# A cached decode attention whose first weight load is issued as two halves, on two queues

## The chip, the cores and the metric

The kernel runs on one core of a Trainium2 chip. The metric is the device time of one execution in microseconds. Before the change it is 2558.99 us, the median of three runs from 2558.98 to 2559.40. "The profile" is one profiled execution of the same program on the chip; its trace holds the start and duration of every instruction and of the DMA engines' packets.

## The reference

Two independent blocks, A and B, of single-token attention over a cache; the outputs stand side by side. For each of them:

```python
B, Sq, D = 8, 1, 1024;  H, Sk, Dh = 32, 4096, 128      # all bf16
q = (x @ wq).reshape(B, Sq, H, Dh).transpose(0, 2, 1, 3)
scores = einsum("bhqd,bhkd->bhqk", q, k_cache) * Dh ** -0.5
o = einsum("bhqk,bhkd->bhqd", softmax(scores), v_cache)
out = o.transpose(0, 2, 1, 3).reshape(B, Sq, H * Dh) @ wo
```

The caches are read once and dominate: 8 x 32 x 4096 x 128 bf16 elements are 268 MB, and there are four of them (K and V of A and B). The weights `wq` and `wo` are 8.39 MB each.

## The kernel before, in words

**Tiles.** Every large load fills one of the three slots of `ring`, an SBUF buffer of 128 partitions and 64 KB per partition and slot. A K or V tile is 8 heads of one batch entry, 8.39 MB; there are 64 K tiles and 64 V tiles. A `wq` fills exactly one slot too: partition p holds the 8 rows 8p to 8p+7 of the matrix, 65,536 contiguous bytes of device memory.

**Order of the loads.** A list `plan` names the loads in order with their slots: `wq` of A (slot 1), K tile 0 (slot 0), `wq` of B (slot 2), then K tile n+1 and V tile n in turn, at the end the two `wo`. All are issued by SyncE, on its DMA queue, and each waits until the slot's last tenant has been used. `load_tiles` issues as far down the list as tenants allow. Between the first load and K tile 0 it also issues the two inputs x (8 partitions, 2 KB each), which lie in slot 2 until they have been transposed.

**The start.** TensorE transposes x once it has landed, VectorE copies the result (L525), TensorE projects it with `wq` of A (`make_q`, L334 and the helper's L36), ScalarE copies the query out of PSUM (L342), TensorE transposes that (L350), VectorE stores it (L354), and ScalarE and TensorE spread the query of one batch entry and 8 heads over the partitions (`qst` L361, `misc` L366, `qbc` L368). Then the loop over the 64 tiles begins.

**The loop.** A K tile is worked in four chunks: VectorE multiplies a chunk with `qbc` in place (`make_mul`, L379), adds the two halves of each row (L384), TensorE adds further with an identity matrix into PSUM (L395, L36), and VectorE reduces to scores (L405). Behind the fourth chunk come maximum, exponent (L417) and the product with V (L434), one tile later. After the last tile, the sums are normalised and multiplied with `wo`.

**How waits are written.** `_Program` keeps one list of operations per engine. An operation that others depend on counts up its engine's semaphore; a load counts up its slot's semaphore (`("t", w)`) by 16. `run(engine, part=(a, b))` emits operations a to b of an engine's list, with waits for the counts that they need. SyncE's first four operations (the first load, the two x, K tile 0) are emitted by a call of its own, ahead of the block in which each engine gets its program.

**Names.** q1 in the profile is SyncE's DMA queue; "SPq" stands for SyncE's issuing of a DMA. A "packet" is what one DMA engine moves at a time; in the large loads it is one partition's 65,536 bytes.

Of the kernel before, what the change touches and what calls it, by code (L numbers as in the profile page):

```python
# [59 lines left out]
class _Program:  # L60
# [13 lines left out]
    def add(self, eng, emit, deps=(), dma_key=None, moves=False):  # L74
        op = _Op(eng, emit, list(deps), dma_key, moves)
        if dma_key is not None:
            self.counts[dma_key] = self.counts.get(dma_key, 0) + 16
            op.token = (dma_key, self.counts[dma_key])
        for d in op.deps:
            if not (d.eng == "pe" and eng == "pe"):  # L80
                d.sig = True
        self.ops[eng].append(op)
        return op
# [32 lines left out]
    def run(self, engname, eng, sems, loop=None, part=(0, None)):  # L116
        ops = self.ops[engname]
        waits, known = self._waits(engname)

        def emit(op, at=lambda base, step: base):  # L120
            ins = op.emit(eng, at) if op.moves else op.emit(eng)
            if op.dma_key is not None:
                ins.then_inc(sems[op.dma_key], 16)
            elif op.sig:
                ins.then_inc(sems[op.eng], 1)

        def straight(lo, hi):
            for op, left in zip(ops[lo:hi], waits[lo:hi]):
                for key, val in left.items():
                    eng.wait_ge(sems[key], val)  # L130
                emit(op)

        start, end = part[0], len(ops) if part[1] is None else part[1]
        ahead = eng.mark_branch_hint_location() if engname in self.ahead else None
        for first, per, rounds in loop or ():
            at = [self.marks[first + per * i][engname] for i in range(rounds + 1)]
            straight(start, at[0])
            self._repeat(engname, eng, sems, ops, waits, known, emit, at, per, rounds, ahead)
            start = at[-1]
        straight(start, end)  # L140
# [32 lines left out]
def _build_kernel(nc, caches, out):  # L173
    B, Sq, D = caches[0][0].shape
    _, H, Sk, Dh = caches[0][1].shape
    NC = len(caches)
    assert B == 8 and Sq == 1 and Dh == 128 and Sk == 4096 and D == 1024 and H % 8 == 0 and 128 % H == 0
    DC = D // 128
# [16 lines left out]
    with es:  # L195
# [36 lines left out]
        sems = {e: es.enter_context(nc.semaphore(f"c_{e}")) for e in ENGINES[1:]}  # L232
# [4 lines left out]
        P = _Program()  # L237
        add = P.add

        def dma(out_ap, in_ap, key, deps, eng="sp"):  # L240
            return add(eng, lambda e: e.dma_start(out_ap, in_ap), deps, dma_key=key)  # L241

        def load_cache(to, n, side, key, deps):
            c = where(n)[0]
            size = HQ * Sk * Dh
            whole = caches[c][side].rearrange("b h s d -> (b h s d)")

            def emit(e, at):
                return e.dma_start(to, whole[bass.ds(at(n % (B * HB) * size, size), size)].rearrange("(p x) -> p x", p=128))
            return add("sp", emit, deps, dma_key=key, moves=True)  # L250
# [23 lines left out]
        opT, opMul, opEacc, opRed, opNgm, opExp = {}, {}, {}, {}, {}, {}  # L274
# [18 lines left out]
        def where(n):  # L293

            return n // (B * HB), n // HB % B, n % HB
# [7 lines left out]
        def load_tiles():  # L303
            while issued[0] < len(plan):
                if issued[0] == 1 and not op_x:
                    op_x.extend(dma(x_sb[:, c, :], caches[c][0].rearrange("b s d -> b (s d)"), ("x", 0), []) for c in range(NC))
                kind, n, w = plan[issued[0]]
                prev = before[issued[0]]
                dep = opUse.get(prev)
                if prev is not None and dep is None:  # L310
                    return
                to, key = ring[:, w, :], ("t", w)
                if kind in ("k", "v"):
                    opT[(kind, n)] = load_cache(to, n, 1 if kind == "k" else 2, key, [dep])
                elif kind == "wq":
                    opT[(kind, n)] = dma(to[:, 0:DC * H * Dh], caches[n][3].rearrange("(p k) n -> p (k n)", k=DC), key, [dep])
                else:
                    from_ = caches[n][4].rearrange("(p r) n -> p (r n)", r=H)
                    for i, (r0, r1) in enumerate(wo_cuts if n == NC - 1 else ((0, H),)):
                        opT[(kind, n, i)] = dma(to[:, r0 * D:r1 * D], from_[:, r0 * D:r1 * D], key if n < NC - 1 else ("w", i), [dep])  # L320
                issued[0] += 1
# [191 lines left out]


        load_tiles()

        def emit_xT(e):
# [14 lines left out]
        for n in range(NQ):  # L532
            P.mark(n)
            for r in range(NR):
                s = n * NR + r
                make_mul(s)
                if s >= LAG:
                    make_red(s - LAG)
                if r == LAG - 1 and n >= 1:
                    make_shift(n - 1)  # L540
                fold = make_fold(s)
                if r == LAG - 1 and n >= 1:
                    make_pm(n - 1)
                if n == 0 and r == NR - 1:
                    for c in range(1, NC):
                        make_q(c)
                        make_qT(c)
                if r == 2 and n >= 1:
                    make_pv(n - 1, 0, RG // 2)
                if r == 3 and n >= 1:  # L550
                    make_pv(n - 1, RG // 2, RG)
                    make_acc(n - 1)
                if r == 2 and n + 1 < NQ:
                    make_stage(n + 1)
                    make_qbc(n + 1)
                make_eacc(s, fold)
                load_tiles()
                if r == 3 and n >= 1:
                    make_ext(n - 1)
        P.mark(NQ)  # L560
        n = NQ - 1
# [4 lines left out]
        make_pv(n, 0, RG)  # L566
        make_acc(n)
        load_tiles()
        make_ext(n)
        make_norm(1)  # L570
# [7 lines left out]
        loops = {"pe": [(1, 2, (NQ - 2) // 2)], "dve": [(3, 2, (NQ - 4) // 2)], "act": [(3, HB, (NQ - 4) // HB)]}  # L578

        P.run("sp", nc.sync, sems, part=(0, 2 + NC))  # L580
        with nc.Block() as block:

            @block.sync
            def _(eng):
                P.run("sp", eng, sems, part=(2 + NC, None))

            @block.tensor
            def _(eng):
                P.run("pe", eng, sems, loops["pe"])

            @block.scalar
            def _(eng):
                P.run("act", eng, sems, loops["act"])

            @block.vector
            def _(eng):
                P.run("dve", eng, sems, loops["dve"])

            @block.gpsimd
            def _(eng):  # L600
                P.run("pool", eng, sems)
# [4 lines left out]
def bass_concat_heads__mha_block_cached__mha_block_cached__decode_kernel(  # L606
    nc, A_x, A_k_cache, A_v_cache, A_wq, A_wo, B_x, B_k_cache, B_v_cache, B_wq, B_wo, out,
):
    caches = [(A_x, A_k_cache, A_v_cache, A_wq, A_wo), (B_x, B_k_cache, B_v_cache, B_wq, B_wo)]
    _build_kernel(nc, caches, out)  # L610
# [28 lines left out]
```

## Time and profile before

| what | value |
|---|---|
| median of three runs | 2558.99 us |
| profiled execution: its span, first to last instruction | 2557.8 us |
| bytes moved by DMA, mean rate | 1107.48 MB, 433 GB/s |
| VectorE busy | 2170.2 us, 85% |
| TensorE busy | 1115.8 us, 44% |
| ScalarE busy | 130.3 us, 5% |
| first load: issued by SyncE at | 0.80 us, landing 22.2 us later |
| first product of VectorE on a K tile | 42.41 us |

The busy share of an engine is an average over the span. In the slices of the page each digit or number is one of 40 equal parts of the span. In a table of windows, a row has the stretch, its length, the busy time of TensorE's matmuls, its weight loads, VectorE, ScalarE and GpSimd with their counts, the granted clock of TensorE, the share of the 16 DMA engines, and GB/s. In a timeline, a row has the start, the duration, the engine, the line and operation with its tiles, and in brackets the idle time ahead of it with what ended it.

### The profile page before, as it was taken

The page shows a single profiled execution, that of the slowest core. Times are in us where ns is not written, and L with a number is a line of the kernel's source. Part 1 is how long each engine was busy: PE and PEld are TensorE (multiplying, and loading weights), DVE is VectorE, ACT ScalarE, POOL GpSimd, SP SyncE. Part 2 cuts the span into 40 slices and gives each one's busy share as a digit, 9 for nine tenths or more (in the row PEclk, how much of TensorE's full clock was granted, in tenths as well). Part 3 has the DMA queues.
Part 4 walks back from the last instruction along what each step waited for, and adds up shares of the span by engine and source line. Part 5 has one row for each costly group of instructions (what it writes and reads, how often), then busy time and mean ns, then how long its engine had stood idle before and what let it go on. Part 6 is the DMA issues. An engine that isn't in the chain of part 4 may idle for free.

```text
span 2557.8 us, 16927 instructions
## 1 busy us (share of the span) xinstructions
PE 1115.8 (44%) x7664; PEld 181.0 (7%) x5808; DVE 2170.2 (85%) x1036; ACT 130.3 (5%) x402; POOL 2.6 (0%) x15
## 2 busy tenths in 40 slices
PE   2443443443444444444444444444444434434444
PEld 0000000000000000000000000000000000000002
DVE  3798898898898898898898888988988988988983
ACT  1100000000000000000000000000000000000000
POOL 0000000000000000000000000000000000000000
PEclk7666776666766666767667767766666767667767
DMA  9999999999999999999999999999999999999999
GB/s 427 427 441 427 442 427 442 427 439 430 438 431 433 436 430 439 429 440 429 440 429 440 430 440 429 440 429 439 429 440 429 440 429 437 431 437 433 435 434 398
DMA packets 19551, 1107.48 MB, mean 433 GB/s; under 512 B 2184, under 2 KB 2248, under 8 KB 2520
## 3 DMA queue, kind: packets, MB, share of 16 engines
q1 hardware_dynamic: 19544, 1107.37, 99.9%
q8 instruction: 6, 0.10, 0.0%
q14 instruction: 1, 0.01, 0.0%
HBM read 1107.33 MB, written 0.03 MB: 433 GB/s over the span
## 4 chain that ended last, share of the span: by engine, by line
DMA 51%; DVE 28%; issue 16%; PE 4%; another core or an unknown queue 0%; ACT 0%; DVEq 0%; SPq 0%
DMA ring<-in_B_k_cache_dram 25%; DMA ring<-in_A_k_cache_dram 25%; DVE ring L379 10%; DVE ring L384 10%; DVE s_sb L405 4%; PE red L36 4%; DVE PM L422 3%; DMA ring<-in_B_wo_dram 2%; PE red L395 1%; DVE rmax L411 1%; DVE rtmp L412 0%; ACT PM L342 0%; DVEq L169 0%; SPq L241 0%
## 5 line engine op out<-in xcount | busy, mean ns | idle before, releaser
L379 DVE TENSOR_TENSOR ring<-ring,qbc 128x8192 bf16<-128x8192 bf16 x256 | 1131.7, 4421 | 300.7 <-DMA ring<-in_B_k_cache_dram 150.9
L395 PE MATMUL red<-ring,ident 128*128 128x512 bf16 x256 | 136.3, 532 | 1382.2 <-DVE ring L384 1382.2
L36 PE MATMUL red<-ring,ident 128*128 128x512 bf16 x1792 | 695.9, 554 | 0.0
L384 DVE TENSOR_TENSOR ring<-ring 128x4096 bf16<-128x4096 bf16 x256 | 582.1, 2274 | 0.0
L405 DVE TENSOR_REDUCE s_sb<-red 128x64 f32<-128x1024 f32 x256 | 311.8, 1218 | 3.4 <-PE red L36 3.4
L434 PE MATMUL pv<-ring,PM 128*32 128x512 bf16 x4096 | 273.8, 414 | 4.7 <-DVE PM L422 4.7
L422 DVE TENSOR_TENSOR PM<-pe,own_h 128x2048 bf16<-128x2048 bf16 x64 | 146.3, 2285 | 0.7 <-ACT pe L417 0.7
L395 PEld LDWEIGHTS red<-ring,ident 128*128 128x128 bf16 x256 | 25.9, 101 | 1653.2 <-DVE ring L384 1653.2
L434 PEld LDWEIGHTS pv<-ring,PM 128*32 128x32 bf16 x4096 | 103.6, 104 | 433.8 <-issue 360.9
L368 ACT ACTIVATE qbc<-misc 128x128 bf16<-128x128 f32 x64 | 17.8, 278 | 1087.0 <-PE misc L366 1087.0
L417 ACT ACTIVATE pe<-s_sb,ngm 128x256 bf16<-128x256 f32 x64 | 32.5, 508 | 465.1 <-DVE ngm L415 465.1
L442 ACT ACTIVATE accS<-pv 128x512 bf16<-128x512 f32 x64 | 38.2, 597 | 352.0 <-PE pv L434 352.0
L451 PEld LDWEIGHTS o<-accS,E 128*32 128x32 bf16 x1024 | 31.3, 100 | 193.3 <-issue 192.1
L451 PE MATMUL o<-accS,E 128*32 128x32 bf16 x1024 | 38.1, 185 | 0.7 <-ACT accS L442 0.7
L457 ACT ACTIVATE o_sb<-o 32x32 f32 (+1 forms) x64 | 11.9, 186 | 450.9 <-PE o L451 443.1
L411 DVE TENSOR_REDUCE rmax<-s_sb 128x1 f32<-128x256 f32 x64 | 26.9, 420 | 2.2
L361 ACT ACTIVATE qst<-qT 128x128 bf16 (+1 forms) x64 | 18.7, 293 | 2.3 <-DVE qT L354 2.3
L525 DVE COPY xT<-misc 128x128 bf16<-128x128 bf16 x1 | 0.2, 225 | 21.9 <-PE misc L521 21.9
L498 PE MATMUL proj<-ring,on_sb 128*32 128x256 bf16 x244 | 10.8, 350 | 15.4 <-DMA ring<-in_A_wo_dram 8.2
L412 DVE TENSOR_SCALAR rtmp<-half,rmax 128x32 f32<-128x32 f32 x64 | 15.5, 241 | 2.3
L354 DVE COPY qT<-misc 128x256 bf16<-128x256 bf16 x2 | 2.6, 1278 | 17.1 <-PE misc L350 17.1
L366 PE MATMUL misc<-ident,qst 128*128 128x128 bf16 x64 | 14.8, 232 | 1.7 <-ACT qst L361 1.7
(37 smaller groups left out, 82.6 us busy)
## 6 DMA issues: line engine op xcount, KB each, us to landing
ring<-in_B_wo_dram SPq DMA_DIRECT2D x1, 5120.0 KB, 32.7
ring<-in_B_wo_dram SPq DMA_DIRECT2D x1, 2048.0 KB, 37.2
ring<-in_B_wo_dram SPq DMA_DIRECT2D x1, 768.0 KB, 38.6
ring<-in_A_k_cache_dram SPq DMA_DIRECT2D x32, 39.7
ring<-in_A_v_cache_dram SPq DMA_DIRECT2D x32, 27.8
ring<-in_B_k_cache_dram SPq DMA_DIRECT2D x32, 39.8
ring<-in_B_v_cache_dram SPq DMA_DIRECT2D x32, 27.8
ring<-in_B_wo_dram SPq DMA_DIRECT2D x1, 256.0 KB, 38.7
```

What stands on the lines that cost most here:

```text
L36: return e.add_instruction(mybir.InstMatmult(name=nc.get_next_instruction_name(), engine=e.engine, start_tensor_calc=start, stop_tensor_ca ...
L361: return e.activation(qst[:, n % 2, :].rearrange("p (j m) -> p j m", m=MP), from_.unsqueeze(2).to_broadcast([128, HQ, MP]), ACTF.Copy)
L379: opMul[s] = add("dve", lambda e: e.tensor_tensor(v, v, qbc[:, n % 2, :].unsqueeze(1).to_broadcast([128, CT, Dh]), ALU.mult), [opT[("k", n ...
L384: return add("dve", lambda e: e.tensor_tensor(v[:, :, 0:64], v[:, :, 0:64], v[:, :, 64:128], ALU.add), [opMul[s]])
L395: i = e.matmul(dst, ident[:], v[:, g, :, j, :], start=True, stop=False)
L405: opRed[s] = add("dve", lambda e: e.tensor_reduce(s_sb[:, n % 2, r * CT:(r + 1) * CT], red_ps[s % 2][:, :].rearrange("p (t w) -> p t w", w ...
L411: m = add("dve", lambda e: e.tensor_reduce(rmax[:], s_sb[:, n % 2, :], AX.X, ALU.max), [opRed[NR * n + NR - 1]])
L417: opExp[n] = add("act", lambda e, at: e.activation(pe[:], s_sb[:, n % 2, :], ACTF.Exp, bias=ngm[:, n % 2:n % 2 + 1], scale=scale, accum_ou ...
L422: opPM[n] = add("dve", lambda e: e.tensor_tensor(PM[:], pe[:].unsqueeze(2).to_broadcast([128, T, HQ]), own_h[:].unsqueeze(1).to_broadcast( ...
L434: i = e.matmul(pv_ps[32 * q:32 * (q + 1), :], PM[:, t:t + 4, :].rearrange("p t j -> p (t j)"), v[:, t * Dh:(t + 4) * Dh], start=(g == 0), ...
L442: opAcc[n] = add("act", lambda e: e.activation(accS[:], pv_ps[:], ACTF.Copy), [opPV[n], _at(opExt, n - 1)])
L451: x = e.matmul(to, E[:, i, PH - 1 - u:PH - 1 - u + MB], accS[:, i * 128 + H * u:i * 128 + H * (u + 1)], start=(i == 0 and u == 0), stop=(i ...
```

## The change

The load of A's `wq` becomes two DMAs. SyncE issues partitions 0 to 63 as its first operation, ScalarE issues partitions 64 to 127 as the first operation of its list, on ScalarE's own DMA queue. Both count up the same semaphore, so that the projection waits for a count of 32. ScalarE's operation is emitted ahead of the block, as SyncE's first four are; the rest of ScalarE's list follows in its block as before. The other edit in `run` keeps the early call from setting a branch mark. Nothing else moves, and the `wq` of B is still one load.

```diff
@@ run
-        ahead = eng.mark_branch_hint_location() if engname in self.ahead else None
+        ahead = eng.mark_branch_hint_location() if engname in self.ahead and loop else None
@@ load_tiles
                 if kind in ("k", "v"):
                     opT[(kind, n)] = load_cache(to, n, 1 if kind == "k" else 2, key, [dep])
+                elif kind == "wq" and n == 0:
+                    from_, rows = caches[n][3].rearrange("(p k) n -> p (k n)", k=DC), 64
+                    for i, eng in enumerate(("sp", "act")):
+                        part = slice(i * rows, (i + 1) * rows)
+                        opT[(kind, n)] = dma(to[part, 0:DC * H * Dh], from_[part, :], key, [dep], eng)
                 elif kind == "wq":
                     opT[(kind, n)] = dma(to[:, 0:DC * H * Dh], caches[n][3].rearrange("(p k) n -> p (k n)", k=DC), key, [dep])
@@ the emission
         P.run("sp", nc.sync, sems, part=(0, 2 + NC))
+        P.run("act", nc.scalar, sems, part=(0, 1))
@@
             @block.scalar
             def _(eng):
-                P.run("act", eng, sems, loops["act"])
+                P.run("act", eng, sems, loops["act"], part=(1, None))
```

On SyncE, at the start of its program (a row has the line, the operation, the tile and its shape; the branch enters the block):

```order
-L241 DMA ring<-in_A_wq_dram 128x32768
+L241 DMA ring<-in_A_wq_dram 64x32768
 L241 DMA ring<-in_A_x_dram 8x1024
 L241 DMA ring<-in_B_x_dram 8x1024
 L249 DMA ring<-in_A_k_cache_dram 128x32768
-L583 UNCONDITIONAL_BRANCH
+L589 UNCONDITIONAL_BRANCH
```

The first load has half its rows here; what follows is the same.

On ScalarE, at the start of the changed program:

```order
L241 DMA ring<-in_A_wq_dram 64x32768
L597 UNCONDITIONAL_BRANCH
L134 BRANCH_PREFETCH_HINT
L347 ACT_TABLE_LOAD
L347 ACTIVATE PM<-o 8x512 x4
L347 ACTIVATE PM<-pv 8x512 x4
```

The DMA is new and stands ahead of the branch into ScalarE's block and of the table load; the rows from the branch on were its first rows before.

## The prediction

> **What bounds the kernel now.** I read the page's slices first, then windows cut to single rounds of packets, then the waits of VectorE and the issue times on SyncE.
>
> ```profile
> span 2557.8 us, 16927 instructions
> ...
> DMA  9999999999999999999999999999999999999999
> GB/s 427 427 441 427 442 427 442 427 439 430 438 431 433 436 430 439 429 440 429 440 429 440 430 440 429 440 429 439 429 440 429 440 429 437 431 437 433 435 434 398
> DMA packets 19551, 1107.48 MB, mean 433 GB/s; under 512 B 2184, under 2 KB 2248, under 8 KB 2520
> ## 3 DMA queue, kind: packets, MB, share of 16 engines
> q1 hardware_dynamic: 19544, 1107.37, 99.9%
> q8 instruction: 6, 0.10, 0.0%
> ```
>
> All sixteen DMA engines are busy in every slice, nearly all bytes go through one queue (q1, SyncE's), and the rate stays between 427 and 442 GB/s up to the last slice, whatever the compute engines do. VectorE, the busiest of those, waits once per tile:
>
> ```profile
> DVE ring L379 <- DMA ring<-in_B_k_cache_dram: 150.9, 32, 4.7
> DVE ring L379 <- DMA ring<-in_A_k_cache_dram: 149.7, 32, 4.8
> ```
>
> That is 64 waits, one for each K tile, of up to 4.7 and 4.8 us. So the time is the moment at which the transfers begin, plus 1107 MB at one pace, plus a short tail. An edit of the first load can act only on the beginning and on the pace of that load; and what it loses there nothing later makes up, because the stream has no gap to give back:
>
> ```profile
> 81.00:1000.00 919.00, 403.82 (x2672) 61.52 (x2011) 806.52 (x382) 43.88 (x142) 0.00 (x0) 0.68 1.00 434
> 1000.00:2535.00 1535.00, 673.95 (x4550) 104.98 (x3443) 1329.38 (x636) 74.26 (x238) 0.00 (x0) 0.69 1.00 434
> ```
>
> The last two columns are the share of the DMA engines and the GB/s: 1.00 and 434 in both stretches. The profiled span of 2557.8 us lies 1.2 us under the median of the runs, 2559.0; I add those 1.2 us again at the end.
>
> **How the first load runs now.** The same columns in short windows; a packet counts whole in the window where it starts:
>
> ```profile
> 1.50:1.80 0.30, 0.00 (x0) 0.00 (x0) 0.30 (x1) 0.00 (x0) 0.23 (x3) 1.00 0.00 0
> 1.80:2.00 0.20, 0.00 (x0) 0.00 (x0) 0.20 (x1) 0.00 (x0) 0.13 (x2) 1.00 9.26 2949
> 2.00:2.20 0.20, 0.00 (x0) 0.00 (x0) 0.09 (x1) 0.03 (x1) 0.20 (x1) 1.00 2.95 983
> 2.20:2.40 0.20, 0.00 (x0) 0.00 (x0) 0.11 (x2) 0.20 (x1) 0.20 (x2) 1.00 2.76 983
> 2.40:2.60 0.20, 0.00 (x0) 0.00 (x0) 0.17 (x3) 0.20 (x1) 0.06 (x2) 1.00 0.91 328
> 2.60:4.70 2.10, 0.00 (x0) 0.00 (x0) 0.13 (x1) 0.85 (x1) 1.12 (x5) 1.00 0.00 0
> 4.70:5.10 0.40, 0.00 (x0) 0.00 (x0) 0.00 (x0) 0.00 (x0) 0.00 (x0) 1.00 1.16 492
> 5.10:5.60 0.50, 0.00 (x0) 0.00 (x0) 0.00 (x0) 0.00 (x0) 0.00 (x0) 1.00 3.94 1704
> ...
> 7.00:8.00 1.00, 0.00 (x0) 0.00 (x0) 0.00 (x0) 0.00 (x0) 0.00 (x0) 1.00 2.42 1049
> ...
> 1.50:20.80 19.30, 0.00 (x0) 0.00 (x0) 1.00 (x4) 1.28 (x1) 1.93 (x10) 1.00 1.04 435
> ```
>
> A row of the weights is 8 x 4096 bf16 = 65,536 bytes. In 7.00:8.00 there start 1.049 MB, which is 16 such packets, one per engine; a share of 2.42 over 1 us and 16 engines is 2.42 us for each. From 1.80 to 2.60 there start 590 + 197 + 197 + 66 KB, again 16 packets; from 2.60 to 4.70 none; from 4.70 to 5.60 the next 16. So the engines go in step: rounds of 16 packets, spread over 0.8 us within a round, and 1.50:20.80 holds the whole load (8.39 MB, 128 packets) in 8 rounds. One packet in 2.42 us is 27.1 GB/s, times sixteen 433 GB/s, the page's mean: each of sixteen lanes runs at one fixed pace.
>
> **The change part by part.**
>
> *Removed and added instructions.* SyncE's first DMA shrinks from 128 rows to 64, and ScalarE issues the other 64 rows on its own queue.
>
> ```profile
> 0.80 0.40 SPq L241 DMA_DIRECT2D ring<-in_A_wq_dram  x1
> 1.26 0.36 SPq L241 DMA_DIRECT2D ring<-in_A_x_dram  x1
> ...
> 2.17 1.28 ACT L342 ACT_TABLE_LOAD   x1 [2.17 <-DVE PM L267]
> ...
> 31.01 2.43 ACT L342 ACTIVATE PM<-o 8x512 bf16<-8x512 f32 x4 [27.56 <-PE pv L36]
> ```
>
> Issuing 128 rows takes SyncE 0.40 us, issuing 8 rows 0.36 us, so a half saves at most 0.04 us there. ScalarE's added issue, about 0.4 us, stands ahead of its table load, which waits until 2.17 us in any case, and behind that ScalarE idles 27.56 us. Both are priced at 0; if that cover were gone, the added issue would cost its own 0.4 us. The wait of the first projection on the load now asks for both halves' counts; it stays one wait.
>
> *The start.* The first packet starts about 1.0 us after the issue (0.80 to 1.80), and the second round follows the first by about 3.0 us instead of 2.42, some 0.6 us for the first data to come. Two queues still have both: priced at 0, with the bounds 1.6 us gained (both gone) and 0.4 us lost (an issue more).
>
> *The pace of the split load.* It is the one term that matters, and no row shows a long load that touches fewer than 128 partitions. The bytes and the packets stay: 128 packets on 16 engines, 8 rounds. What changes is where a round writes. If each half is spread over all 16 engines, every engine holds 4 packets for partitions 0 to 63 on one queue and 4 for 64 to 127 on the other, and takes them in turn; in step as they are, all 16 engines write into one half of the partitions in the same round, then all into the other. Bounds: if an engine's own 27.1 GB/s is the limit, a round still takes 2.42 us and the term is 0. If the lanes end at the partitions, sixteen lanes for 128, half the partitions take half the pace, and two engines share a lane: with a distance d between the two, a packet takes 2 x 2.42 - d, since only the time in which both write is halved. By the spread of the rounds d lies between 0 and 0.8 us; a round costs 1.62 to 2.42 us more, eight rounds 13.0 to 19.4 us. A load is whole only when its slowest engines are through, so a pair close together decides: with d = 0.2, 8 x 2.22 = 17.8 us. I take the second, because of the fixed pace: 434 GB/s from 81 to 1000 and again to 2535 us, with everything that the compute engines do meanwhile, looks like sixteen equal lanes that a 128-row load happens to fill exactly. It is an inference; the row does not say at which end the lane is narrow.
>
> [...]
>
> *What follows on the path.* Everything behind the split load in the queues shifts by the same amount. The steps beside it have slack:
>
> ```profile
> 24.63 0.35 SPq L241 DMA_DIRECT2D ring<-in_B_wq_dram  x1
> 31.01 0.33 SPq L249 DMA_DIRECT2D ring<-in_A_k_cache_dram  x1
> 71.45 0.33 SPq L249 DMA_DIRECT2D ring<-in_A_v_cache_dram  x1
> ...
> 38.86 0.28 ACT L368 ACTIVATE qbc<-misc 128x128 bf16<-128x128 f32 x1 [0.38 <-PE misc L366]
> ...
> 42.41 4.43 DVE L379 TENSOR_TENSOR ring<-ring,qbc 128x8192 bf16<-128x8192 bf16 x1 [4.28 <-DMA ring<-in_A_k_cache_dram]
> ...
> 82.48 4.42 DVE L379 TENSOR_TENSOR ring<-ring,qbc 128x8192 bf16<-128x8192 bf16 x1 [3.90 <-DMA ring<-in_A_k_cache_dram]
> ```
>
> The broadcast query is ready at 38.86 + 0.28 = 39.14, 3.27 us before the first K tile at 42.41; a later weight load delays the tile as much, so the order stays. The first V load, issued at 71.45, finds the second K tile still under way (it lands by 82.48). The queues don't run dry, and the shift arrives whole at the end.
>
> Sum: 2557.8 + 17.8 (pace) + 0 (issues) + 0 (start) = 2575.6 of span, plus 1.2: **2576.8 us**, 0.7% slower.
>
> **Rivals.**
>
> 1. *The engines set the pace* (not slower): a lane is narrow at the engine, and which partitions a round writes is indifferent; or the halves come to different engines, or engines take the queues in opposite order, so that each round spreads over all partitions. Eight rounds of 2.42 us stay, the start moves between 1.6 us less and 0.4 more: 2557.4 to 2559.4, most likely 2559.0. For it: 16 x 27.1 gives the rate without a word on partitions. Against it: the rounds are in step, so opposite order needs an accident in all pairs. [...]
>
> 2. *Half the price*: lanes end at the partitions, but engines drift apart within the load, so that from the middle on they write opposite halves. Four dear rounds: 4 x 2.22 = 8.9 us, 2568. For it: a spread of 0.8 us exists from the first round. Against it: with equal shares a distance keeps its size.
>
> 3. *The halves don't go in turn*: ScalarE's half is served after the first K tile, or issued late. The weights are then whole near 42 instead of 23 us (the inputs x, queued behind them, let the transposes start at 23.5), 19 us later; 3.27 us of slack goes first, then what the first V load has, 80 - 71.45 = 8.5 us; the queue stays empty for the remaining 7 us: 2566. Against it: both issues come before 1.7 us, while the first packets start at 1.80.
>
> **How the numbers follow.** Forecast 0.53, rival 1 0.41, rival 2 0.04, rival 3 0.02. The forecast's own range is 2572 to 2578.5 (13.0 to 19.4 us more). Cases of both kinds hold much of the chance, so the range that holds 8 in 10 must reach from rival 1's middle to the dear end: 2558.2 to 2579. What a measurement here can tell from no change is about 0.2%, 5.1 us. Faster by that much would need the first load 5.1 us shorter, beyond the 1.6 us that the start could give; I leave it 0.01 of rival 1's 0.41. Within: the other 0.40. Slower: the forecast with rivals 2 and 3, 0.59.
>
> **What would show it.** In short windows of the changed kernel's first 45 us: packets of about 4.6 us instead of 2.42 and a rate near 225 GB/s until about 39 us, with two queues in the table of queues; VectorE's first product at about 60 instead of 42.41; from there on the old distances, 434 GB/s and a share of 1.00. It is wrong if the first load still goes at 435 GB/s and VectorE starts near 42.4 (rival 1), if the pace recovers midway (rival 2), or if a gap in the DMA share opens near 80 us (rival 3).

## The result and the profile after

The changed kernel takes 2578.98 us (median of four runs, 2578.70 to 2579.16) against 2559.06 us for the kernel before: 19.9 us or 0.8% slower, ratio 1.0078 with a 95% interval of 1.0063 to 1.0092. The forecast was 2576.8, its own range 2572 to 2578.5: the result lies 0.5 us above that range, and inside the wider one that ends at 2579.

The page of the changed kernel, the same parts as of before:

```profile
span 2577.8 us, 16958 instructions
...
DMA  9999999999999999999999999999999999999999
GB/s 292 424 438 439 425 437 439 429 434 438 436 428 436 437 428 436 438 427 436 439 426 436 439 429 435 437 435 430 436 436 429 436 437 428 436 439 426 436 439 395
...
## 3 DMA queue, kind: packets, MB, share of 16 engines
q1 hardware_dynamic: 19480, 1103.18, 99.2%
q10 hardware_dynamic: 80, 4.19, 0.8%
```

The first of the forty slices is the one that fell, from 427 to 292 GB/s; the others stay between 424 and 439 up to the last, and the engines count as busy throughout. "Busy" here hides the loss: an engine counts as busy for the whole of a packet, and the windows below show a share of 1.00 at 212 GB/s as at 434. q10 is ScalarE's queue, with half a weight (4.19 MB).

The changed kernel in windows (the last two columns are the share of the engines and GB/s; a packet counts whole where it starts):

```profile
1.80:2.10 0.30, 0.00 (x0) 0.00 (x0) 0.28 (x1) 0.00 (x0) 0.23 (x2) 1.00 0.00 0
2.10:2.40 0.30, 0.00 (x0) 0.00 (x0) 0.12 (x2) 0.23 (x1) 0.30 (x2) 1.00 13.19 2840
...
6.50:7.50 1.00, 0.00 (x0) 0.00 (x0) 0.00 (x0) 0.00 (x0) 0.00 (x0) 1.00 4.93 1049
7.50:11.40 3.90, 0.00 (x0) 0.00 (x0) 0.00 (x0) 0.00 (x0) 0.00 (x0) 1.00 0.00 0
11.40:12.40 1.00, 0.00 (x0) 0.00 (x0) 0.00 (x0) 0.00 (x0) 0.00 (x0) 1.00 4.93 1049
12.40:16.30 3.90, 0.00 (x0) 0.00 (x0) 0.00 (x0) 0.00 (x0) 0.00 (x0) 1.00 0.00 0
16.30:17.30 1.00, 0.00 (x0) 0.00 (x0) 0.00 (x0) 0.00 (x0) 0.00 (x0) 1.00 4.93 1049
...
1.50:41.00 39.50, 0.00 (x0) 0.00 (x0) 0.99 (x4) 1.28 (x1) 1.92 (x10) 1.00 1.00 212
...
100.00:1020.00 920.00, 405.31 (x2676) 61.66 (x2011) 806.45 (x382) 43.83 (x142) 0.00 (x0) 0.68 1.00 434
1020.00:2555.00 1535.00, 674.03 (x4550) 105.12 (x3439) 1329.17 (x636) 74.19 (x238) 0.00 (x0) 0.68 1.00 434
```

Rounds of 16 packets as before, but each packet takes 4.93 us instead of 2.42, with nothing starting between two rounds; the load goes at 212 GB/s. In the trace's packet records the 16 packets of a round all belong to one queue, and the queue changes from round to round, so a round writes one half of the partitions. Behind the load the 434 GB/s of before are back and stay.

VectorE and the issues of the changed kernel, in time:

```profile
0.80 0.56 ACTq L241 DMA_DIRECT2D ring<-in_A_wq_dram  x1
...
0.80 0.60 SPq L241 DMA_DIRECT2D ring<-in_A_wq_dram  x1
1.46 0.74 SPq L241 DMA_DIRECT2D ring<-in_A_x_dram  x1
...
62.60 4.43 DVE L384 TENSOR_TENSOR ring<-ring,qbc 128x8192 bf16<-128x8192 bf16 x1 [5.12 <-DMA ring<-in_A_k_cache_dram]
...
102.46 4.43 DVE L384 TENSOR_TENSOR ring<-ring,qbc 128x8192 bf16<-128x8192 bf16 x1 [2.95 <-DMA ring<-in_A_k_cache_dram]
```

(Line 384 of the changed kernel is line 379 of the kernel before.) The first product moves from 42.41 to 62.60 us, 20.2 later, and the product on the second K tile from 82.48 to 102.46, 20.0 later. The span grows by 20.0, so all of the loss has been made before these instructions and nothing behind the second tile gives any of it back.

### The profile page after: what moved, and what is told of

Same layout as the page of the kernel before. It is cut to its first block, busy times and chain, and to the rows that moved or that the text cites. A ratio compares the mean times of both kernels' runs of the same rounds, so it can differ in the third digit from the quotient of the medians.

```text
span 2577.8 us, 16958 instructions
## 1 busy us (share of the span) xinstructions
PE 1115.4 (43%) x7664; PEld 181.0 (7%) x5808; DVE 2169.9 (84%) x1036; ACT 130.1 (5%) x402; POOL 2.6 (0%) x15
## 3 DMA queue, kind: packets, MB, share of 16 engines
q10 hardware_dynamic: 80, 4.19, 0.8%
## 4 chain that ended last, share of the span: by engine, by line
DMA 51%; DVE 27%; issue 17%; PE 5%; ACT 0%; another core or an unknown queue 0%; DVEq 0%; SPq 0%
DMA ring<-in_B_k_cache_dram 25%; DMA ring<-in_A_k_cache_dram 23%; DVE ring L384 10%; DVE ring L389 10%; PE red L36 3%; DVE PM L427 3%; DVE s_sb L410 2%; DMA ring<-in_B_x_dram 2%; DMA ring<-in_B_wo_dram 2%; PE red L400 1%; DVE rmax L416 1%; ACT PM L347 0%; DVE rtmp L417 0%; PE o L339 0%
```

## The experiments

The loss could have two causes that look alike in the changed kernel: the half of the partitions that a round writes (the partition theory, on which the forecast stood), or engines that serve two queues in turn and lose time at each change (the queue theory). Each experiment edits one load, in all but one of them the first, and leaves the rest. Where SyncE issues more or fewer loads at the start, the count of operations that it emits ahead of its block is moved with them, and those lines are left out of the edits below.

**One queue, the same halves.** From the kernel before:

```diff
+                elif kind == "wq" and n == 0:
+                    from_, rows = caches[n][3].rearrange("(p k) n -> p (k n)", k=DC), 64
+                    for i in range(128 // rows):
+                        part = slice(i * rows, (i + 1) * rows)
+                        opT[(kind, n)] = dma(to[part, 0:DC * H * Dh], from_[part, :], key, [dep])
```

> The same two halves of 64 partitions, both issued by SyncE on its one queue, one behind the other; the rest as before. Partition theory (64 partitions take half the pace, whichever queue): packets of about 4.9 us, first load some 39 us long, 2579 us (19 to 21 more than before). Queue theory (an engine that alternates between two queues loses a packet's time at each change): packets of 2.42 us, 2559 us, as before.

Measured: 2580.21 us, ratio 1.0083 (1.0066 to 1.0100). Its windows:

```profile
1.50:42.30 40.80, 0.00 (x0) 0.00 (x0) 0.99 (x4) 1.28 (x1) 1.93 (x10) 1.00 0.99 206
```

The loss is there without a second queue. It is even 1.2 us larger, 206 GB/s for 212. Its third and its fifth round:

```profile
11.70:13.00 1.30, 0.00 (x0) 0.00 (x0) 0.00 (x0) 0.00 (x0) 0.00 (x0) 1.00 3.95 807
...
22.00:23.30 1.30, 0.00 (x0) 0.00 (x0) 0.00 (x0) 0.00 (x0) 0.00 (x0) 1.00 3.78 807
```

A share of 3.95 over 1.3 us is 5.14 us a packet, 3.78 is 4.91. The fifth round is the first one of the second half.

**Two queues, split by columns.** From the changed kernel:

```diff
-                    from_, rows = caches[n][3].rearrange("(p k) n -> p (k n)", k=DC), 64
+                    from_, cols = caches[n][3].rearrange("(p k) n -> p (k n)", k=DC), DC * H * Dh // 2
                     for i, eng in enumerate(("sp", "act")):
-                        part = slice(i * rows, (i + 1) * rows)
-                        opT[(kind, n)] = dma(to[part, 0:DC * H * Dh], from_[part, :], key, [dep], eng)
+                        part = slice(i * cols, (i + 1) * cols)
+                        opT[(kind, n)] = dma(to[:, part], from_[:, part], key, [dep], eng)
```

> Two DMAs on two queues as in the change, but split by columns: each has all 128 partitions and 32 KB of each partition's 64 KB. Partition theory: each packet of 32 KB takes 1.21 us, first load 19.4 us as before, 2559 us within 1. Queue theory: each change of queue costs, packets of about 2.4 us for 32 KB, about 2579 us.

Measured: 2559.03 us, ratio 1.000 (0.9991 to 1.001). One round of it, 16 packets of 32 KB in 1 us:

```profile
4.50:5.50 1.00, 0.00 (x0) 0.00 (x0) 0.00 (x0) 0.00 (x0) 0.00 (x0) 1.00 1.21 524
```

1.21 us is half of 2.42: two queues cost nothing that shows. The queue theory falls, and the second queue brings nothing either (2559.03 us, for 2558.93 of the kernel before).

**Quarters.** As the first experiment with `rows = 32`, four DMAs.

> The first load as four DMAs of 32 partitions on SyncE's queue. If the pace goes with the number of partitions: a quarter of 433 GB/s, 77 us for the load, about 2617 us. If 32 partitions reach as many lanes as 64 do: half the pace, packets of 4.9 us, about 2579 us. Queue theory: 2559 us.

Measured: 2579.86 us, ratio 1.0082 (1.0061 to 1.0102). Rounds three to six:

```profile
11.00:13.00 2.00, 0.00 (x0) 0.00 (x0) 0.00 (x0) 0.00 (x0) 0.00 (x0) 1.00 2.57 524
16.20:18.20 2.00, 0.00 (x0) 0.00 (x0) 0.00 (x0) 0.00 (x0) 0.00 (x0) 1.00 2.56 524
21.20:23.20 2.00, 0.00 (x0) 0.00 (x0) 0.00 (x0) 0.00 (x0) 0.00 (x0) 1.00 2.47 524
26.20:28.20 2.00, 0.00 (x0) 0.00 (x0) 0.00 (x0) 0.00 (x0) 0.00 (x0) 1.00 2.57 524
```

A share over 2 us, so a packet takes twice that: 5.14, 5.12, 4.94, 5.14 us. Quarters are no slower than halves on one queue (5.14 us, and 4.91 where the second half begins): 32 neighbouring partitions get the pace that 64 get, so the pace doesn't go with the count of partitions.

**Even and odd partitions.** From the changed kernel:

```diff
-                    from_, rows = caches[n][3].rearrange("(p k) n -> p (k n)", k=DC), 64
+                    from_ = caches[n][3].rearrange("(p k) n -> p (k n)", k=DC)
                     for i, eng in enumerate(("sp", "act")):
-                        part = slice(i * rows, (i + 1) * rows)
-                        opT[(kind, n)] = dma(to[part, 0:DC * H * Dh], from_[part, :], key, [dep], eng)
+                        opT[(kind, n)] = dma(to[i:128:2, 0:DC * H * Dh], from_[i:128:2, :], key, [dep], eng)
```

> Two queues of 64 partitions each as in the change, but SyncE's half is the even partitions and ScalarE's the odd ones, so that each half reaches from 0 to 127. If the pace goes with the number of partitions in a DMA (64): packets of 4.9 us, 2579 us. If lanes belong to blocks of neighbouring partitions and the engines write in different blocks within a round: 2.42 us, 2559 us. If engines that go in step meet in the same blocks even so: something between, up to 2579 us.

Measured: 2559.23 us, ratio 1.0001 (0.9990 to 1.0012).

```profile
7.55:8.55 1.00, 0.00 (x0) 0.00 (x0) 0.00 (x0) 0.00 (x0) 0.00 (x0) 1.00 2.42 1049
```

The round shown has 16 packets at 2.42 us. If the queues go in turn here as they do in the changed kernel, it is 64 even or 64 odd partitions alone, and 64 partitions do take the whole pace if they lie spread out. The split is free in any case.

**Writing or reading.** The halves differ in device memory too. Two kernels cross the sides. The first reads the contiguous halves of the weights and writes them to even and odd partitions, the second reads even and odd rows and writes them to partitions 0 to 63 and 64 to 127:

```diff
-                        opT[(kind, n)] = dma(to[part, 0:DC * H * Dh], from_[part, :], key, [dep], eng)
+                        opT[(kind, n)] = dma(to[i:128:2, 0:DC * H * Dh], from_[part, :], key, [dep], eng)
```
```diff
-                        opT[(kind, n)] = dma(to[part, 0:DC * H * Dh], from_[part, :], key, [dep], eng)
+                        opT[(kind, n)] = dma(to[part, 0:DC * H * Dh], from_[i:128:2, :], key, [dep], eng)
```

> Two queues of 64 rows as in the change, read from the same contiguous halves of the weights in device memory, but SyncE's half is written to the even partitions and ScalarE's to the odd ones. The weights then stand in other partitions than the query's, so the projection is of permuted weights and the output is not the reference's; the work is the same. If the loss is made where the packets are written (blocks of neighbouring partitions): 2.42 us a packet, 2559 us within 1. If it is made where they are read (halves of the weights in device memory): 4.9 us a packet, 2579 us.

> The mirror: even rows of the weights' layout read by SyncE's DMA and written to partitions 0 to 63, odd rows by ScalarE's to 64 to 127 (again weights permuted over the partitions, so another output, the same work). Loss at the writing side: 4.9 us a packet, 2579 us. Loss at the reading side: 2.42 us, 2559 us.

Measured: 2559.30 us, ratio 1.0002 (0.9991 to 1.0013), for the first, and 2578.95 us, ratio 1.0078 (1.0049 to 1.0108), for the second. A round of the first, then of the second (a share over 2 us):

```profile
7.50:8.50 1.00, 0.00 (x0) 0.00 (x0) 0.00 (x0) 0.00 (x0) 0.00 (x0) 1.00 2.42 1049
```
```profile
6.00:8.00 2.00, 0.00 (x0) 0.00 (x0) 0.00 (x0) 0.00 (x0) 0.00 (x0) 1.00 2.45 524
```

2.42 and 4.90 us: reading contiguous or alternate rows makes no such difference; the loss goes with the partitions written.

**The second weight instead of the first.** The loop of the first experiment under `n == 1`; the first load stays whole.

> The first load whole as before; instead the second weight load (B's, issued at 24.6 us into a busy queue) as two halves of 64 partitions on SyncE's queue. Partition theory, with the stream as the only bound: the same 20 us at another place, 2578 to 2580 us. If a loss in the middle is made up by the work that waits there: under 2565 us. Queue theory: 2559 us.

Measured: 2580.89 us, ratio 1.0086 (1.0065 to 1.0106), 22.0 more than before. Nothing of a loss in the middle is made up. The K tile behind this load reaches VectorE at 103.35 us instead of 82.48, 20.9 later, and the tile behind that comes 21.3 later (142.39 for 121.07 us). The profiled execution is 21.7 longer; the rest I could not place.

```profile
103.35 4.42 DVE L384 TENSOR_TENSOR ring<-ring,qbc 128x8192 bf16<-128x8192 bf16 x1 [5.80 <-DMA ring<-in_A_k_cache_dram]
```

**The first load whole, on ScalarE's queue.** From the changed kernel:

```diff
-                    from_, rows = caches[n][3].rearrange("(p k) n -> p (k n)", k=DC), 64
-                    for i, eng in enumerate(("sp", "act")):
-                        part = slice(i * rows, (i + 1) * rows)
-                        opT[(kind, n)] = dma(to[part, 0:DC * H * Dh], from_[part, :], key, [dep], eng)
+                    opT[(kind, n)] = dma(to[:, 0:DC * H * Dh], caches[n][3].rearrange("(p k) n -> p (k n)", k=DC), key, [dep], "act")
```

> The first load whole (128 partitions) but issued by ScalarE on its queue; x and the first K tile go on SyncE's queue beside it. Partition theory: both queues in turn at 2.42 us a packet, 434 GB/s throughout; the weights are then whole near 39 instead of 22 us, the query near 55, VectorE starts near 55 instead of 42.4, and the first V load goes out near 85, some 5 us after the queue ran dry: 2562 to 2567 us. Queue theory: packets of 4.9 us while both queues hold work, about 2579 us or more.

Measured: 2564.76 us (2564.17 to 2565.99), ratio 1.0024 (1.0012 to 1.0035). A round, the rates of longer stretches, and the steps that were late:

```profile
4.80:5.80 1.00, 0.00 (x0) 0.00 (x0) 0.00 (x0) 0.00 (x0) 0.00 (x0) 1.00 2.42 1049
...
1.50:41.00 39.50, 2.50 (x32) 1.45 (x28) 1.22 (x5) 1.28 (x1) 1.92 (x10) 1.00 1.00 426
...
80.00:100.00 20.00, 8.54 (x74) 1.45 (x34) 13.52 (x10) 5.51 (x11) 0.00 (x0) 0.67 0.87 365
...
82.00:88.00 6.00, 1.48 (x28) 0.18 (x8) 0.99 (x1) 4.31 (x8) 0.00 (x0) 0.97 0.87 339
...
85.00:88.00 3.00, 0.00 (x0) 0.00 (x0) 0.00 (x0) 2.88 (x6) 0.00 (x0) 0.95 0.93 393
...
53.23 4.42 DVE L381 TENSOR_TENSOR ring<-ring,qbc 128x8192 bf16<-128x8192 bf16 x1 [1.11 <-ACT qbc L370]
...
83.52 0.33 SPq L249 DMA_DIRECT2D ring<-in_A_v_cache_dram  x1
```

The round shown is at full pace, 2.42 us a packet, and 1.50:41.00 goes at 426 GB/s, yet 5.8 us are lost. The weights and the first K tile shared the engines, so the projection came late (its first product at 39.60 us instead of 24.91), VectorE waited for the query instead of the tile, and the first V load was issued at 83.52 instead of 71.45, after the queue had run dry: between 80 and 100 us the engines work 0.87 of the time. This is the third rival's chain, and it costs more than the slack alone gives: the V load is issued 12.1 us late, 8.5 of them are covered by the prediction's estimate (80 - 71.45), which leaves 3.6. Part of the rest is in the restart. By the windows, 13 packets start between 82 and 85 us (6.00 x 339 less 3.00 x 393 is 855 KB), and they take about 3.0 us each instead of 2.42 (0.87 x 6.00 x 16 less 0.93 x 3.00 x 16 is 38.9 us). From the issue to the first packet the kernel before needs 1.0 us (0.80 to 1.82); I estimate the same here. The fourth K tile is 4.8 us late (164.52 for 159.77) and the profiled execution 5.1; what lies between these and the 5.8 of the median is open.

**Quarters in another order.** The quarters of above with `for i in (0, 2, 1, 3)`.

> The four quarters on SyncE's one queue again, in the order 0-31, 64-95, 32-63, 96-127, so that the half of the partitions changes after every second round instead of once. If the time that the changed kernel gets back in each round (4.92 us a round, where one queue needs 5.13) comes from the change of half: the three rounds that end in a change take about 4.9 us, the others 5.13, and the total is 0.4 us under the quarters in order, 2579.4 us. If it comes from having two queues: all rounds 5.13, no less than the quarters in order, 2579.9 us. If two engines met by their distance in time, rounds would differ from engine to engine.

Measured: 2579.24 us, ratio 1.0079 (1.0049 to 1.0108), 0.6 us under the quarters in order (two runs of each; two more rounds at 0.2 us less would make 0.4). Rounds two to seven:

```profile
6.40:7.40 1.00, 0.00 (x0) 0.00 (x0) 0.00 (x0) 0.00 (x0) 0.00 (x0) 1.00 5.13 1049
11.55:12.55 1.00, 0.00 (x0) 0.00 (x0) 0.00 (x0) 0.00 (x0) 0.00 (x0) 1.00 4.92 1049
16.45:17.45 1.00, 0.00 (x0) 0.00 (x0) 0.00 (x0) 0.00 (x0) 0.00 (x0) 1.00 5.13 1049
21.55:22.55 1.00, 0.00 (x0) 0.00 (x0) 0.00 (x0) 0.00 (x0) 0.00 (x0) 1.00 4.93 1049
26.45:27.45 1.00, 0.00 (x0) 0.00 (x0) 0.00 (x0) 0.00 (x0) 0.00 (x0) 1.00 5.12 1049
31.60:32.60 1.00, 0.00 (x0) 0.00 (x0) 0.00 (x0) 0.00 (x0) 0.00 (x0) 1.00 4.93 1049
```

A packet takes 5.13 us when the one ahead of it went to the same half, and 4.92 when the half has changed. I had expected the saving in the packet ahead of a change; it is in the one behind. The changed kernel changes half in every round, so its packets from the second round on are of the second kind (4.92 to 4.95 us in its packet records), by the order of the writes and not by having two queues.

## Why the prediction was right or wrong

**Right: the mechanism and the path.** The pace of the split load was the term that decided; rounds in step write one half of the partitions at a time; the stream has no gap to give the loss back (20.0 us late at the second K tile, 20.0 at the end of the span). The column split, the even and odd split and the crossed pair leave no other reading of which half is meant: that of the partitions written. The prediction had no row for it and called the step from "sixteen equal lanes" an inference; it came out, but not as it was drawn. Not 64 partitions as such are slow, but 64 neighbours (4.93 us a packet in the changed kernel, 2.42 in the even and odd split), and a lane is not a block of eight neighbours either: 32 of them would then reach four lanes and take a quarter of the pace, and the quarters took half (5.14 us a packet, as with halves on one queue). In the quarters a change from 0-31 to 64-95 saves 0.2 us (4.92 for 5.13), and one from 0-31 to 32-63 does not (5.14). Which partitions share a lane the runs show no further.

**Wrong: the size of that term.** 17.8 us were forecast with bounds of 13.0 and 19.4; the span grew by 20.0, above the upper bound. The step that failed is "a packet takes 2 x 2.42 - d": 4.64 us were forecast, 4.92 to 4.93 measured. It fails on two counts. It lets two engines on a lane share it without loss; but a packet takes 5.13 us, not 4.84, so the shared pace is 6% lower in total than half and half. Why, the runs don't say.

And d is not the distance of two engines' starts. In the changed kernel every packet of rounds two to eight takes 4.92 to 4.95 us by the packet records, though the starts within a round lie 0.9 us apart; in the quarters in another order the sixteen packets of a round behind a change take 4.92 to 4.93 us on average, and those of the other rounds shown 5.12 to 5.13. With a distance, the engine that comes last would have saved its time ahead of the change, and pairs with other distances would have saved other amounts. That the saving is near the 0.2 that I had taken for d is an accident.

With what was measured, 4.92 for 2.42 us, eight rounds give 8 x 2.50 = 20.0. That this meets the span so exactly is partly luck too: by the packet records the first round costs only 1.7 us more (4.84 for 3.18), the other seven 2.5 each, the load starts 0.3 later, and the first round of the K tile behind it takes 0.4 longer (2.98 for 2.55).

**Wrong in a small thing: the issue.** I said that 64 rows take at most 0.04 us less to issue than 128, from 0.40 and 0.36 us. They take more: 0.60 and 0.56 us, and the first packets start after 2.10 us instead of 1.80. In the even and odd split, whose packets are at full pace, that is all that is left of the change, and its median is 0.25 us above the kernel before, too little to tell from none. The bounds that I gave the start (1.6 us gained to 0.4 lost) held.

**The rivals.** The first (engines set the pace) is refuted: a packet takes 2.42 or 5.13 us by where it is written. Half of its wording came true elsewhere: in the even and odd split each round does reach over all the partitions, and costs nothing (2559.23 us). Its 0.41 beside the forecast's 0.53 says what the page of before could tell: it did not part the two, and only the runs did. Whether two blocks of 64 neighbours would run at full pace with the engines writing both in the same round was not tried. The second fails: the rounds stay in step and at 4.92 to 4.95 us up to the eighth. The third did not occur here; the first load on ScalarE's queue shows its chain at work, at 5.8 us, for a V load that was 12.1 us late.

## What to carry to other kernels

In a kernel like this one, cut a large load so that each piece still reaches partitions from all over, by columns or by a stride over the partitions: halves by columns, or even and odd partitions, were free here (2559.03 and 2559.23 us in all, 1.21 us for 32 KB and 2.42 us for 64 KB a packet), while blocks of 64 neighbouring partitions ran at half the pace, on two queues (4.93 us a packet) and on one (5.14), and so did blocks of 32 on one queue (5.14). A second queue gave no bandwidth where all sixteen engines were busy (2559.03 us with the column split, 2558.93 without), and a busy share of 1.00 said nothing about the pace (212 and 434 GB/s under the same share): read the time of one packet. Where the transfers were the bound from start to end, a loss in a load reached the end undiminished: 20.0 us of span for the first load, 21.7 for the second.

## What the runs showed of the hardware

- A packet of 64 KB takes 5.13 us where all sixteen engines write into one block of 32 or 64 neighbouring partitions, and 2.42 us in a load of all 128 partitions or in one split by even and odd partitions. 5.13 is 6% more than 2 x 2.42; why, the runs don't say.
- A packet whose predecessor wrote the other half takes about 4.9 instead of 5.13 us (4.92 to 4.95 for all 112 packets of rounds two to eight in the changed kernel); why, the runs don't say.
- A DMA of 64 rows takes longer to issue (0.55 to 0.60 us, contiguous or every second row) than one of the same weights with all 128 rows (0.39 to 0.40 us), on SyncE and on ScalarE. The cause is open.
- In the changed kernel the queues of SyncE and ScalarE take turns on the engines, round by round. Loads on both queues showed no cost of that where the pieces reach all over the partitions: 1.21 us for 32 KB, 2.42 us for 64 KB.
